# Another order of ScalarE, VectorE, GpSimd and transfer requests in one unit of work and in units 1 to 6 of a fused attention and feed-forward kernel

## The chip, the cores and the metric

The kernel runs on one core of one Trainium2 chip. A core has five engines that each work through a queue of their own in order: TensorE (PE in the profile; PEld are its weight loads), VectorE (DVE), ScalarE (ACT), GpSimd (POOL) and SyncE (SP), which here issues nearly all transfers. They meet through semaphores. The metric is the time of one execution on the device in microseconds; lower is better. The kernel before takes 911.8 us (median of three runs, 911.2 to 911.83).

## The reference

Attention with pooled keys and values, and behind it a feed-forward layer, all in float32. There are 8 batches, 8 heads, 576 tokens and 64 elements per head; the layer has 512 inputs and 2048 hidden elements.

```python
k_p = k.reshape(B, H, 72, 8, D).mean(axis=3)
v_p = v.reshape(B, H, 72, 8, D).mean(axis=3)
scores = scale * np.matmul(q, k_p.transpose(0, 1, 3, 2))
scores = scores - np.max(scores, axis=-1, keepdims=True)
attn = np.exp(scores)
attn = attn / (np.sum(attn, axis=-1, keepdims=True) + 1e-09)
x = np.matmul(attn, v_p).transpose(0, 2, 1, 3).reshape(B * S, H * D)
h = x @ w_in
s = np.sin(alpha * h)
g = h + s * s / (alpha + 1e-09)
out = g @ w_out
```

## The kernel before

The program has two stages. In the first, unit u (0 to 7) computes the hidden layer of batch u, and in the gaps between its products it carries the attention of batch u + 1. In the second stage `outputs` multiplies g, which was parked in device memory (`g_bridge`), with w_out. Both matrix products use seven block products in place of eight (Strassen and Winograd): sums of weight blocks (`as1`, `as2`, `as4`, and `a21` overwritten with a difference) and sums of x blocks (the `home` tiles) are made by GpSimd and VectorE, and TensorE multiplies them.

`hidden` (L1030) works in four parts J, each a quarter of the hidden elements. A part owns four banks of PSUM, b1, b5, b6 and b7. After the first product ScalarE copies b1 into b6 (`copy(G.b6, G.b1)`), TensorE goes on adding to b6, ScalarE copies b6 into b7, and so on: in the profile these are the `ACT COPY PS<-PS 128x512` rows, and TensorE can't start the products `PS<-home,as` on b6 before the copy is there. Then ScalarE takes sin and square (`s`), VectorE adds h, p5 and s into `h`, and SP stores `h` to `g_bridge`. In units 1 to 6 the products 1 and 5 of the later parts are themselves split once more (`inner_product`, L1146); its step d is an add on VectorE, `PS<-PS,m` in the profile, for which the next product waits.

`first_batch` (L1192) does the attention of batch 0 and the first weights, ahead of unit 0. `carry(u)` (L1286) gives the list of what unit u carries, by slot: for u = 0 among other things `sum_v_rows`, the rest of batch 0's attention, `pairs_q` for batch 1, `load_w_in_part` 2 and 3, the weight sums `combine_w_in` of parts 1 to 3, the transposes of queries and keys (`q_t`, `k_t`), `two_scores` (products), `two_shifts` (row maxima and subtraction, `mx` and `ex` in the profile), `exp`, `norm` (sums `sm` on VectorE, the scaling `ex<-ex,sm` on GpSimd), `turn` (VectorE's transposes `tr<-ex`), `move` (the transfers `aM<-tr`) and `turn_q` (the queries of the last tokens, transfers `q<-tr`). `pool_k` and `pool_v` are GpSimd's sums over eight rows (`kvin<-kvin`, `kp`, `vm`). `pairs_q` (L315) copies the queries of one batch on ScalarE, five copies of 128x512 (`q<-q`), from a tile that one request of 1024 KB brings. `refine` improves a reciprocal of alpha on VectorE (`t`, `c`), which ScalarE's square reads.

The order of the work is written in a table. Between `begin` and `flush` every operation is only recorded (class `Order`, L30; this is why all rows of the profile have the line L156). `flush` (L139) computes which operation needs which, and then sorts the queue of each engine but TensorE by a number; TensorE keeps the order of the program text. The number is `unit * 5406` plus the entry of the table `PLAN` for the operation's key: the part (`0` for unit 0, `u` for units 1 to 6, `7`, `8` for units on their own, `a` for the first batch) and the label of the function that `carry` named, followed by the running number of the operation under this key. The entries read like times in hundredths of a microsecond. SP is a queue like the others; a request waits until the one eight places before it has landed.

Of the kernel before, what the change touches and what calls it, by code (L numbers as in the profile page):

```python
# [189 lines left out]
0.: 0 0 0 0 2004 0 0 0 0 0 0 0 0 2591 0 0 0 0 2633 2696 2690 2746 2694 4180 0 0 0 0 2990 2765 2695 0 0 0 0 4153 2764 4401 0 0 0 0 2763 2775 5075 4488 2772 4489 4208 4777 5545 5542 0 0 0 0 4486 0 0 0 0 0 0 0 0 5073 0 0 0 0 5074 5077 5078 5136 5128 4798 0 0 0 0 4778 5409 5572 0 0 0 0 4796 5357 5425 0 0 0 0 5441 5440 5444 5442 5445 5789 4850 4851 5556 5752 0 0 0 0 5377 0 0 0 0 0 0 0 0 5443 0 0 0 0 5529 5702 5615 5794 5792 4861 0 0 0 0 4848 5852 5795 0 0 0 0 4856 5798 6403 0 0 0 0 5800 5797 8483 7999 5855 5799 4866 8188 5773 5766 0 0 0 0 5850 0 0 0 0 0 0 0 0 6301 0 0 0 0 6335 8687 8002 8723 8716 8405 0 0 0 0 8176 8733 8863 0 0 0 0 8200 8734 9669 0 0 0 0 8732 9668 8997 9675 9343 9670 9566 9825 10996 11157  # L190
0.sum_v_rows : 0 0 0 0 0 0 0 0 1974
0.rest_q : 0 0 0 0 1975
0.a_head : 0 0 0 0 1976 0 0 0 0 2136 0 0 0 0 2002
0.values : 0 0 0 0 0 0 2137 2144 2006 2007
0.score : 0 0 0 0 0 0 0 0 2189 2204 2182 2208
0.sums_of_x : 2164 2206 8538 8549
0.load_w_in_part : 1725 2031 2255 1019 5540 683 1828 1956
0.pairs_q : 2299 2612 2003 2005 2755
0.call : 5175 3333
0.combine_w_in : 3139 3158 3332 3331 3336 3338 3501 3383 3834 5996 5169 8465  # L200
0.q_t : 0 0 0 0 2213 0 0 0 0 2222 0 0 0 0 4487 0 0 0 0 5071 0 0 0 0 5070
0.k_t : 0 0 0 2219 0 0 0 8471
0.two_scores : 0 0 0 0 0 0 0 0 0 0 0 0 0 0 0 0 0 0 0 0 0 0 0 0 0 0 0 0 0 0 0 0 4127 4194 3335 4124 4125 4128 0 0 0 0 0 0 0 0 0 0 0 0 0 0 0 0 0 0 0 0 0 0 0 0 0 0 0 0 0 0 0 0 0 0 0 0 0 0 0 0 4211 4774 4214 4776
0.load_v : 5536 5537 1606 4600 660 507 3399 3602 3718
0.<lambda> : 3161 3335 3337 3367 8457 8458 8459 7637 8463 8464 0 0 0 0 0 0 0 0 0 0 0 0 7576 8000 6318 6990
0.exp : 2675 5072 5076 5120 5336
0.load_q : 5538 5546 5543
0.norm : 4511 4787 3660 4784 4797 3752 4811 4812 4427 4801 4803 3793
# [20 lines left out]
u.load_k : 376 5758  # L229
u.pool_k : 3087 3088 3091 8469 8471 8477  # L230
u.move : 5779 5774 5773 5769 5764 5766 5771 5767 5777 5775 5776 5762 5778 5763 5768 5770
u.turn_q : 7643 7606 7969 6332 6330 6292 6328 6255 6334 6333 6335 6339 6336 6340 5895 6338 6331 6426 6472
u.all_values : 0 0 0 0 0 0 0 0 0 0 8016 0 0 0 0 0 0 0 0 0 0 0 0 0 0 0 0 0 0 8512 8520 8579 8519 8521 8564 8577 8557 8551
u.k_t : 0 0 0 8267
# [1486 lines left out]
```

## Time and profile before

| | |
|---|---|
| median of three runs | 911.8 us |
| profiled execution | 915.4 us |
| its span, first to last instruction | 913.4 us |
| mean granted TensorE clock | 0.996 |
| TensorE busy | 898.0 us, 98% |
| VectorE busy | 667.4 us, 73% |
| ScalarE busy | 457.9 us, 50% |
| GpSimd busy | 196.6 us, 22% |

The span is the time between the first and the last instruction of the profiled execution; the rest of its 915.4 us lies around it. In a row of the timeline stand start and duration in microseconds, the engine, the operation, the tile written and the tiles read (numbers left out), the shape, how many instructions of the kind came in a row, and in brackets how long the engine had been idle before and what released it. The releaser is inferred. A row that covers several instructions (x8) has the time from the start of the first to the end of the last. The view by windows gives the busy time of TensorE, its weight loads, VectorE, ScalarE and GpSimd in each stretch, with the number of instructions, and then the granted clock of TensorE (1.00 is full), the share of the transfer engines, and GB/s.

### The profile page before, as it was taken

The page shows a single profiled execution, that of the slowest core. Times are in us where ns is not written, and L with a number is a line of the kernel's source. Part 1 is how long each engine was busy: PE and PEld are TensorE (multiplying, and loading weights), DVE is VectorE, ACT ScalarE, POOL GpSimd, SP SyncE. Part 2 cuts the span into 40 slices and gives each one's busy share as a digit, 9 for nine tenths or more (in the row PEclk, how much of TensorE's full clock was granted, in tenths as well). Part 3 has the DMA queues.
Part 4 walks back from the last instruction along what each step waited for, and adds up shares of the span by engine and source line. Part 5 has one row for each costly group of instructions (what it writes and reads, how often), then busy time and mean ns, then how long its engine had stood idle before and what let it go on. Part 6 is the DMA issues. An engine that isn't in the chain of part 4 may idle for free.

```text
span 913.4 us, 18293 instructions
## 1 busy us (share of the span) xinstructions
PE 898.0 (98%) x7122; PEld 818.5 (90%) x7122; DVE 667.4 (73%) x1029; ACT 457.9 (50%) x1112; POOL 196.6 (22%) x232
## 2 busy tenths in 40 slices
PE   8899999999999999999999999999999999999998
PEld 5687888888888788888888899999999999999998
DVE  7465866858587585764279589979787878878884
ACT  5486876877768687787796631111111112112111
POOL 4579754424445144220000000000000000000000
PEclk9899999999999999999999999999999999999999
DMA  9947676586666766343727237352527262626211
GB/s 259 228 131 195 193 209 202 158 229 187 194 184 172 206 191 184 122 133 127 266 93 248 93 103 227 115 145 70 181 39 191 57 183 77 183 66 195 66 39 40
DMA packets 128748, 141.14 MB, mean 155 GB/s; under 512 B 46920, under 2 KB 95704, under 8 KB 128664
## 3 DMA queue, kind: packets, MB, share of 16 engines
q1 hardware_dynamic: 125880, 137.88, 52.3%
q10 hardware_dynamic: 2784, 2.11, 0.9%
q8 instruction: 56, 0.92, 0.4%
q14 instruction: 28, 0.23, 0.1%
HBM read 75.37 MB, written 47.19 MB: 134 GB/s over the span
## 4 chain that ended last, share of the span: by engine, by line
PE 91%; DMA 3%; DVE 2%; SPq 2%; issue 0%; ACT 0%; DVEq 0%
PE PS L156 91%; SPq L156 2%; DMA a<-in_moe_w_in_dram 2%; DMA home<-in_k_dram 1%; DMA kvin<-in_v_dram 1%; DVE h L156 1%; DVE tr L156 0%; DMA q<-tr 0%; DVE ex L156 0%; DVE PS L156 0%; DVE mx L156 0%; DVE sm L156 0%; ACT L156 0%; ACT q L156 0%; DVE c L156 0%
## 5 line engine op out<-in xcount | busy, mean ns | idle before, releaser
L156 ACT COPY PS<-PS 128x144 f32<-128x144 f32 (+4 forms) x312 | 114.4, 369 | 296.6 <-PE PS L156 282.2
L156 PE MATMUL PS<-home,a 128*128 128x256 f32 (+1 forms) x1080 | 253.2, 376 | 1.4 <-DVE h L156 0.5
L156 PEld LDWEIGHTS PS<-home,a 128*128 128x128 f32 x1080 | 196.8, 191 | 30.1 <-issue 4.6
L156 PE MATMUL PS<-home,as 128*128 128x256 f32 (+1 forms) x792 | 188.6, 374 | 4.0 <-ACT PS L156 4.0
L156 PEld LDWEIGHTS PS<-home,as 128*128 128x128 f32 x792 | 144.4, 192 | 21.9 <-ACT PS L156 4.4
L156 PE MATMUL PS<-s,wb 128*128 128x144 f32 x896 | 119.1, 286 | 0.0
L156 ACT ACTIVATE s<-s,c 128x256 f32<-128x256 f32 (+1 forms) x216 | 116.7, 577 | 4.5 <-DVE c L156 2.1
L156 PEld LDWEIGHTS PS<-s,wb 128*128 128x128 f32 x896 | 113.7, 190 | 0.1
L156 POOL TENSOR_TENSOR cc<-cc,cb 128x576 f32<-128x576 f32 x1 | 2.0, 1983 | 504.9 <-DVE cb L156 504.9
L156 ACT ACTIVATE s<-PS,al 128x256 f32<-128x256 f32 x144 | 64.5, 471 | 33.5 <-PE PS L156 33.3
L156 DVE TENSOR_TENSOR h<-PS,s 128x512 f32<-128x512 f32 x72 | 49.0, 681 | 36.3 <-ACT s L156 35.9
L156 ACT ACTIVATE s<-h,al 128x256 f32<-128x256 f32 x144 | 68.6, 507 | 12.8 <-DVE h L156 12.7
L156 PE MATMUL PS<-s,a 128*128 128x144 f32 x512 | 73.2, 286 | 0.0
L156 PE MATMUL PS<-r,wb 128*128 128x144 f32 x512 | 73.2, 286 | 0.0
L156 DVE TENSOR_TENSOR h<-PS,p 128x512 f32<-128x512 f32 x72 | 49.0, 680 | 25.0 <-ACT p L156 12.7
L156 POOL TENSOR_TENSOR kvin<-kvin 96x768 f32<-96x768 f32 (+3 forms) x42 | 66.0, 1573 | 5.5 <-DMA kvin<-in_v_dram 4.8
L156 PEld LDWEIGHTS PS<-r,wb 128*128 128x128 f32 x512 | 67.1, 190 | 0.1
L156 PEld LDWEIGHTS PS<-s,a 128*128 128x128 f32 x512 | 67.0, 190 | 0.0
L156 DVE TENSOR_TENSOR h<-h,s 128x1024 f32<-128x1024 f32 x36 | 50.2, 1394 | 18.9 <-ACT s L156 18.9
L156 PE MATMUL PS<-x,wb 128*128 128x144 f32 x384 | 54.9, 286 | 0.0
L156 PE MATMUL PS<-s,we 128*128 128x144 f32 x384 | 54.9, 286 | 0.0
L156 POOL TENSOR_TENSOR ex<-ex,sm 128x576 f32<-128x576 f32 (+1 forms) x28 | 35.3, 1272 | 86.3 <-DVE sm L156 75.0
(170 smaller groups left out, 1309.2 us busy)
## 6 DMA issues: line engine op xcount, KB each, us to landing
g_bridge<-h SPq DMA_DIRECT2D x72, 512.0 KB
r<-g_bridge SPq DMA_DIRECT2D x31, 1152.0 KB
out_dram<-o SPq DMA_DIRECT2D x122, 72.0 KB
kvin<-in_k_dram SPq DMA_DIRECT2D x14, 576.0 KB
q<-in_q_dram SPq DMA_DIRECT2D x7, 1024.0 KB
kvin<-in_v_dram SPq DMA_DIRECT2D x14, 512.0 KB
aM<-tr SPq DMA_DIRECT2D x54, 92.0 KB
aM<-tr SPq DMA_DIRECT2D x54, 88.0 KB
```

Of the source, the lines that this page charges most:

```text
L156: t.f(*t.a, **t.k)
```

## The change

Only entries of `PLAN` change: those of part `0` (unit 0) and of part `u` (units 1 to 6). The entries of the first batch's own part `a`, of units 7 and 8 and of the second stage stay. So the same instructions run on the same data; TensorE's program is the same, instruction by instruction, and the queues of ScalarE, VectorE, GpSimd and SP have another order from the point where unit 0 is mixed into the first batch, through unit 6. A selection of the changed lines follows; all other labels under `0` and `u` have new entries too, in the same manner.

```diff
--- before
+++ after
@@ -187,51 +187,51 @@
-0.: 0 0 0 0 2004 0 0 0 0 0 0 0 0 2591 0 0 0 0 2633 2696 2690 2746 2694 4180 0 0 0 0 2990 2765 2695 0 0 0 0 4153 2764 4401 0 0 0 0 2763 2775 5075 4488 2772 4489 4208 4777 5545 5542 0 0 0 0 4486 0 0
...
-0.load_w_in_part : 1725 2031 2255 1019 5540 683 1828 1956
-0.pairs_q : 2299 2612 2003 2005 2755
-0.combine_w_in : 3139 3158 3332 3331 3336 3338 3501 3383 3834 5996 5169 8465
-0.q_t : 0 0 0 0 2213 0 0 0 0 2222 0 0 0 0 4487 0 0 0 0 5071 0 0 0 0 5070
-0.load_v : 5536 5537 1606 4600 660 507 3399 3602 3718
-0.exp : 2675 5072 5076 5120 5336
-0.norm : 4511 4787 3660 4784 4797 3752 4811 4812 4427 4801 4803 3793
-0.turn : 4814 4799 4810 4813 4838 4828 4821 4815 4849 4816 4807 4809
-0.inner_w_in : 8468 8490 8496 8500 5172 8471 5173 8481 8462 8472 8488 13874 3551 6818 8498 8483 8461 8492 8489 13884 8460 8474 8466 13864
-u.: 0 0 0 0 3590 0 0 0 0 4268 0 0 0 0 4270 4271 4543 4542 4452 0 0 0 0 0 0 4541 4401 0 0 0 0 4544 4474 5061 5025 0 0 4545 0 0 0 4475 0 0 4478 5098 5307 0 0 0 0 0 0 5305 5253 5308 5311 5309 5306
...
-u.inner_x : 3074 3089 3085 3093 3073 3076 3079 3078
-u.load_v : 354 348 347 133 138 135 3070 3080 3081
-u.norm : 4477 4499 3095 4479 4481 3096 4480 5279 8457 5241 5242 3097
-u.turn : 4563 5283 5281 5251 5287 5328 5286 5680 5285 5379 5280 6064
-u.pool_v : 3061 3064 3067 3069
-u.pool_k : 3087 3088 3091 8469 8471 8477
...
+0.: 0 0 0 0 2019 0 0 0 0 0 0 0 0 2024 0 0 0 0 2913 3322 3421 3323 3866 3963 0 0 0 0 2221 3347 3870 0 0 0 0 2757 3975 3873 0 0 0 0 3372 3724 5445 5443 3958 3871 4146 4307 4958 4692 0 0 0 0 3872 0 0
...
+0.load_w_in_part : 1702 412 2367 1749 4594 4503 2068 2255
+0.pairs_q : 2023 2022 2025 2342 3324
+0.combine_w_in : 3105 3107 3117 3116 3109 3111 3145 3143 3157 3344 3341 3345
+0.q_t : 0 0 0 0 2173 0 0 0 0 2210 0 0 0 0 3582 0 0 0 0 3941 0 0 0 0 4009
+0.load_v : 4495 4560 4825 4643 4631 4511 3242 3335 3339
+0.exp : 2668 5441 5444 5453 5451
+0.norm : 4154 4265 3222 4266 4293 3231 4725 4726 3332 4436 4469 3331
+0.turn : 4801 4800 4502 4803 4802 4804 4788 4794 4795 4798 4799 4756
+0.inner_w_in : 3110 3367 3334 8466 3115 3185 8470 8464 3237 3333 8500 8469 3148 3338 8487 8492 3352 8499 8472 8501 8465 8474 3376 8486
+u.: 0 0 0 0 4277 0 0 0 0 4283 0 0 0 0 4289 4290 4294 4424 4476 0 0 0 0 0 0 4293 4295 0 0 0 0 4296 4444 5355 4965 0 0 4297 0 0 0 4445 0 0 4478 5353 5358 0 0 0 0 0 0 5013 5351 5362 5361 5359 5360
...
+u.inner_x : 3056 3067 3062 3082 3057 3074 3061 3079
+u.load_v : 5544 5556 152 163 161 149 3088 3090 3091
+u.norm : 4477 4479 3085 4480 4667 3092 4481 4482 3087 4484 4487 3089
+u.turn : 4483 4486 4674 4673 4488 4489 4671 4669 4670 4672 5161 5326
+u.pool_v : 3055 3065 3069 3076
+u.pool_k : 3083 3084 8458 8457 8459 8460
...
```

In words, what moves in the stretch of the first batch and unit 0:

- On ScalarE the copies b6 from b1 (2004, now 2019) and b7 from b6 (2591, now 2024) of the first part: the former stood behind the first `pairs_q` copy, and now stands ahead of all of them.
- On SP the request for the queries of batch 1 goes from place 22 to 19; four requests for value rows (`vr`, 64 KB each) go from places 11, 14, 23 and 34 to 32, 36, 37 and 41; the weight requests between them close up and change places.
- On VectorE several `ex<-PS,mx` and `h<-PS,p` move ahead of `h<-h,s` and of row maxima, and the refinement of the reciprocal moves back.
- On GpSimd small sums of weight blocks for the inner products of unit 1 (`q<-a`, `q<-as`, `last<-a`) are spread over unit 0 among the weight sums, and value sums (`vr`, `vz`) move back.

In units 1 to 6 the reciprocals of the softmax sums and some of the transposes `tr<-ex` change places with the h adds on VectorE, single sin and square operations change places on ScalarE, and on GpSimd the pooling of the next values (`kvin<-kvin`) moves from early in a unit to between the softmax scalings.

More of the change, by code (lines that the diff above doesn't have):

```diff
@@ L191 @@
[L191 to L196, printed above, removed]
-0.load_w_in_part : 1725 2031 2255 1019 5540 683 1828 1956
-0.pairs_q : 2299 2612 2003 2005 2755
-0.call : 5175 3333
-0.combine_w_in : 3139 3158 3332 3331 3336 3338 3501 3383 3834 5996 5169 8465
-0.q_t : 0 0 0 0 2213 0 0 0 0 2222 0 0 0 0 4487 0 0 0 0 5071 0 0 0 0 5070
@@ L202 @@
-0.k_t : 0 0 0 2219 0 0 0 8471
-0.two_scores : 0 0 0 0 0 0 0 0 0 0 0 0 0 0 0 0 0 0 0 0 0 0 0 0 0 0 0 0 0 0 0 0 4127 4194 3335 4124 4125 4128 0 0 0 0 0 0 0 0 0 0 0 0 0 0 0 0 0 0 0 0 0 0 0 0 0 0 0 0 0 0 0 0 0 0 0 0 0 0 0 0 4211 4774 4214 4776
-0.load_v : 5536 5537 1606 4600 660 507 3399 3602 3718
-0.<lambda> : 3161 3335 3337 3367 8457 8458 8459 7637 8463 8464 0 0 0 0 0 0 0 0 0 0 0 0 7576 8000 6318 6990
-0.exp : 2675 5072 5076 5120 5336
-0.load_q : 5538 5546 5543
-0.norm : 4511 4787 3660 4784 4797 3752 4811 4812 4427 4801 4803 3793
@@ L209 @@
-0.load_k : 5547 5548
-0.two_shifts : 4775 4785
-0.turn : 4814 4799 4810 4813 4838 4828 4821 4815 4849 4816 4807 4809
-0.norm_rest : 2608 4126 4951 3334 3160
-0.move : 5697 5558 5554 5751 5553 5552 5617 5550 5557 5551 5549 5555 5796 5793 5791 5790
-0.a_rest : 0 0 0 0 0 5856
-0.inner_w_in : 8468 8490 8496 8500 5172 8471 5173 8481 8462 8472 8488 13874 3551 6818 8498 8483 8461 8492 8489 13884 8460 8474 8466 13864
-0.turn_q : 4873 4870 7364 5756 5758 5755 5759 5761 5762 5765 5763 5769 5757 5771 5770 5764 5767 5772 5768
@@ L228 @@
-u.pool_v : 3061 3064 3067 3069
-u.load_k : 376 5758
-u.pool_k : 3087 3088 3091 8469 8471 8477
[L231 to L234, printed above, removed]
+0.: 0 0 0 0 2019 0 0 0 0 0 0 0 0 2024 0 0 0 0 2913 3322 3421 3323 3866 3963 0 0 0 0 2221 3347 3870 0 0 0 0 2757 3975 3873 0 0 0 0 3372 3724 5445 5443 3958 3871 4146 4307 4958 4692 0 0 0 0 3872 0 0 0 0 0 0 0 0 5442 0 0 0 0 5446 5449 5447 5450 5448 4414 0 0 0 0 4268 5463 5455 0 0 0 0 4309 5454 5456 0 0 0 0 5461 5458 5466 5460 5465 5459 4806 4808 5553 5554 0 0 0 0 5452 0 0 0 0 0 0 0 0 5457 0 0 0 0 5462 5468 5467 5470 5472 4809 0 0 0 0 4805 5475 5473 0 0 0 0 4807 5486 5481 0 0 0 0 5474 5471 5493 5494 5478 5477 4810 4814 5566 5577 0 0 0 0 5476 0 0 0 0 0 0 0 0 5483 0 0 0 0 5488 5485 7852 5490 7859 6412 0 0 0 0 4815 9692 9684 0 0 0 0 5606 9690 9686 0 0 0 0 9673 9685 9691 9693 9694 9687 9482 9619 10966 10965
@@ new lines @@
+0.sum_v_rows : 0 0 0 0 0 0 0 0 2015
+0.rest_q : 0 0 0 0 2018
+0.a_head : 0 0 0 0 2016 0 0 0 0 2136 0 0 0 0 2017
+0.values : 0 0 0 0 0 0 2143 2153 2020 2021
+0.score : 0 0 0 0 0 0 0 0 2154 2164 2156 2158
+0.sums_of_x : 2170 2155 8255 8520
+0.load_w_in_part : 1702 412 2367 1749 4594 4503 2068 2255
+0.pairs_q : 2023 2022 2025 2342 3324
+0.call : 3337 3108
+0.combine_w_in : 3105 3107 3117 3116 3109 3111 3145 3143 3157 3344 3341 3345
+0.q_t : 0 0 0 0 2173 0 0 0 0 2210 0 0 0 0 3582 0 0 0 0 3941 0 0 0 0 4009
@@ new lines @@
+0.k_t : 0 0 0 2214 0 0 0 7334
+0.two_scores : 0 0 0 0 0 0 0 0 0 0 0 0 0 0 0 0 0 0 0 0 0 0 0 0 0 0 0 0 0 0 0 0 2224 2668 2220 3781 2222 2580 0 0 0 0 0 0 0 0 0 0 0 0 0 0 0 0 0 0 0 0 0 0 0 0 0 0 0 0 0 0 0 0 0 0 0 0 0 0 0 0 4151 4300 4308 4361
+0.load_v : 4495 4560 4825 4643 4631 4511 3242 3335 3339
+0.<lambda> : 3336 3340 3343 3348 3346 3347 7189 3368 3378 3386 0 0 0 0 0 0 0 0 0 0 0 0 5489 5487 5491 5484
+0.exp : 2668 5441 5444 5453 5451
+0.load_q : 5101 4628 4662
+0.norm : 4154 4265 3222 4266 4293 3231 4725 4726 3332 4436 4469 3331
@@ new lines @@
+0.load_k : 4654 5544
+0.two_shifts : 4156 4267
+0.turn : 4801 4800 4502 4803 4802 4804 4788 4794 4795 4798 4799 4756
+0.norm_rest : 2219 2223 3287 3342 3113
+0.move : 5547 5550 5546 5234 5342 5375 5549 5310 5545 5551 5552 5548 5479 5482 5469 5464
+0.a_rest : 0 0 0 0 0 5480
+0.inner_w_in : 3110 3367 3334 8466 3115 3185 8470 8464 3237 3333 8500 8469 3148 3338 8487 8492 3352 8499 8472 8501 8465 8474 3376 8486
+0.turn_q : 4812 4813 4811 5556 5562 5560 5561 5565 5559 5564 5563 5575 5571 5570 5568 5572 5573 5574 5576
@@ new lines @@
+0.all_values : 0 0 0 0 0 0 0 0 0 0 5492 0 0 0 0 0 0 0 0 0 0 0 0 0 0 0 0 0 0 7848 7905 7875 7714 7779 5917 9668 9672 7867
+u.sums_of_x : 3292 3125 7984 8493
+u.: 0 0 0 0 4277 0 0 0 0 4283 0 0 0 0 4289 4290 4294 4424 4476 0 0 0 0 0 0 4293 4295 0 0 0 0 4296 4444 5355 4965 0 0 4297 0 0 0 4445 0 0 4478 5353 5358 0 0 0 0 0 0 5013 5351 5362 5361 5359 5360 4490 4536 5643 5639 4952 0 0 0 0 5352 5354 0 0 5357 0 0 5356 0 0 0 4485 0 0 0 0 5366 5367 5363 5370 5369 4668 0 0 0 0 5364 5365 0 0 4643 6143 6441 0 0 5368 0 0 0 4666 0 0 4996 6542 6437 0 0 0 0 0 0 6468 6439 6621 6628 6541 6504 5519 5845 5784 5782 6164 0 0 0 0 6424 6467 0 0 6469 0 0 6458 0 0 0 5501 0 0 0 0 6623 6619 6620 6627 6624 5820 0 0 0 0 6622 6626 0 0 5588 6631 6632 0 0 6625 0 0 0 5794 0 0 5896 6639 6640 0 0 0 0 0 0 6630 6636 7357 6951 6635 6638 7569 7979 5802 10951 6629 0 0 0 0 6633 6634 0 0 6785 0 0 6637 0 0 0 7458 0 0 0 0 6642 6641 7412 9679 7535 8323 0 0 0 0 7982 9682 9680 0 0 0 0 8170 9685 9684 0 0 0 0 9687 9688 9692 9686 9690 9691 9848 9849 10963 10965
@@ new lines @@
+u.two_scores : 0 0 0 0 0 0 0 0 0 0 0 0 0 0 0 0 0 0 0 0 0 0 0 0 0 0 0 0 0 0 0 0 3201 3234 3212 3244 3223 3256 0 0 0 0 0 0 0 0 0 0 0 0 0 0 0 0 0 0 0 0 0 0 0 0 0 0 0 0 0 0 0 0 0 0 0 0 0 0 0 0 3748 3805 3773 4351
+u.inner_x : 3056 3067 3062 3082 3057 3074 3061 3079
+u.two_shifts : 3798 3799
+u.load_v : 5544 5556 152 163 161 149 3088 3090 3091
+u.load_q : 5650 5638 5783
+u.exp : 4292 4291 4504 4464
+u.norm : 4477 4479 3085 4480 4667 3092 4481 4482 3087 4484 4487 3089
+u.turn : 4483 4486 4674 4673 4488 4489 4671 4669 4670 4672 5161 5326
@@ L235 @@
+u.pool_v : 3055 3065 3069 3076
+u.load_k : 383 5640
+u.pool_k : 3083 3084 8458 8457 8459 8460
+u.move : 5657 5652 5647 5649 5656 5651 5645 5641 5710 5654 5653 5642 5655 5644 5646 5648
+u.turn_q : 7974 7971 7976 5791 5792 5790 5787 5788 5794 5793 5795 5800 5796 5797 5798 5799 5801 5785 5786
+u.all_values : 0 0 0 0 0 0 0 0 0 0 6643 0 0 0 0 0 0 0 0 0 0 0 0 0 0 0 0 0 0 9676 7517 9673 9678 9672 9675 9674 9677 9681
+u.k_t : 0 0 0 8476
 7.: 42508 42507 42505 42506 0 0 0 0 42507 0 0 0 0 0 0 0 0 42508 0 0 0 0 42509 42510 42511 42514 42515 42390 0 0 0 0 42388 42512 42520 0 0 0 0 42389 42513 42523 0 0 0 0 42517 42519 42521 42525 42522 42528 42391 42393 42510 42509 0 0 0 0 42516 0 0 0 0 0 0 0 0 42524 0 0 0 0 42526 42530 42531 42536 42535 42395 0 0 0 0 42392 42534 42539 0 0 0 0 42394 42537 42543 0 0 0 0 42550 42538 42547 42546 42552 42541 42399 42396 43585 43586 0 0 0 0 42542 0 0 0 0 0 0 0 0 42549 0 0 0 0 42545 42553 42555 42554 42563 42404 0 0 0 0 42398 42560 42562 0 0 0 0 42403 46237 42566 0 0 0 0 46281 42565 46238 42567 46325 46236 46819 46817 43587 43588 0 0 0 0 42564 0 0 0 0 0 0 0 0 46239 0 0 0 0 46419 46421 46706 46807 46809 46823 0 0 0 0 46818 46808 46756 0 0 0 0 46820 46811 46810 0 0 0 0 46814 46813 46817 46812 46816 46815 46826 46827 43589 43590
```

8 lines of the change are left out of this document (removed).

## The prediction

> **What bounds the kernel now.** I read the page first: which engine is busy, and the clock row.
>
> ```profile
> PE 898.0 (98%) x7122; PEld 818.5 (90%) x7122; DVE 667.4 (73%) x1029; ACT 457.9 (50%) x1112; POOL 196.6 (22%) x232
> ...
> PEclk9899999999999999999999999999999999999999
> ```
>
> TensorE is busy for 898.0 of 913.4 us, so all other engines together can give back 15.4 us, and nothing that leaves the TensorE program alone can give more, except through the clock. The clock row has one digit of 8, early. The view by windows says where the idle time and the low clock are (window, its length, PE busy; PEclk is the third figure from the end of a row).
>
> ```profile
> 0.00:20.00 20.00, 17.75 (x224) 10.79 (x224) 13.95 (x35) 11.05 (x22) 6.95 (x16) 1.00 0.97 264
> 20.00:40.00 20.00, 15.29 (x90) 11.08 (x91) 7.44 (x17) 8.01 (x18) 13.37 (x13) 0.84 1.06 250
> 40.00:120.00 80.00, 78.69 (x712) 66.12 (x711) 55.33 (x94) 61.56 (x129) 63.06 (x76) 1.00 0.65 176
> 120.00:400.00 280.00, 277.25 (x2325) 237.58 (x2324) 196.07 (x337) 213.28 (x514) 110.85 (x126) 1.00 0.64 182
> 400.00:880.00 480.00, 479.88 (x3538) 464.02 (x3539) 377.11 (x521) 159.15 (x416) 0.36 (x1) 1.00 0.45 135
> ```
>
> Idle are 2.25 us in the first 20, 4.71 in the next 20, 1.31 from 40 to 120 (unit 0), 2.75 from 120 to 400 (units 1 to 5), 0.12 after that. The 20 to 40 slice also ran at a mean clock of 0.84. TensorE's waits, from the view of waits (total, times, longest):
>
> ```profile
> PE PS L156 <- ACT PS L156: 4.0, 1, 4.0
> PE PS L156 <- DVE PS L156: 2.5, 6, 0.4
> ```
>
> One wait of 4.0 us on ScalarE stands out; then come six of about 0.42 us on VectorE, and a few single ones. These two rows lie in the part of the program that the change reorders. ScalarE's timeline shows the large one (start, duration, idle time before it and its releaser), and TensorE's what it did to the products:
>
> ```profile
> 25.80 0.58 ACT L156 COPY aM<-PS 64x512 f32<-64x512 f32 x1 [0.29 <-PE PS L156]
> 32.91 0.62 ACT L156 COPY q<-q 128x512 f32<-128x512 f32 x1 [6.54 <-DMA a<-in_moe_w_in_dram]
> 33.54 0.57 ACT L156 COPY PS<-PS 128x512 f32<-128x512 f32 x1
> ```
>
> ```profile
> 25.60 1.89 PE L156 MATMUL PS<-home,as 128*128 128x256 f32 x8
> 27.42 1.09 PE L156 MATMUL PS<-aM,vm 64*64 64x512 f32 x8
> 28.44 1.13 PE L156 MATMUL PS<-aM,vz 32*128 32x512 f32 x4
> 29.50 0.72 PE L156 MATMUL PS<-h,q 64*64 64x72 f32 x16
> 34.17 3.78 PE L156 MATMUL PS<-home,as 128*128 128x256 f32 x8 [3.95 <-ACT PS L156]
> 37.74 3.19 PE L156 MATMUL PS<-home,a 128*128 128x256 f32 x8
> 40.77 0.49 PE L156 MATMUL PS<-ident,q 128*128 128x128 f32 x3
> ```
>
> From the timeline of VectorE and of SP's requests, two rows more:
>
> ```profile
> 29.65 0.76 DVE L156 SCALAR_TENSOR_TENSOR home<-PS,home 128x256 f32<-128x256 f32 x2 [3.60 <-PE PS L156]
> ...
> 32.86 0.37 SPq L156 DMA_DIRECT2D a<-in_moe_w_in_dram  x1
> ```
>
> TensorE is done with everything it can do at 30.21 and waits for a bank copy, b6 from b1 (`PS<-PS`, 0.57 us). That copy's source was written by the eight products that started at 25.60; it could run then. But it is queued on ScalarE behind a copy of the second batch's queries (`pairs_q`, 0.62 us), and ScalarE stands 6.54 us until the 1 MB query transfer has landed. The row names a transfer of weights; by the code, the copy reads the queries, and the request on SP that waits for the query transfer (eight requests behind it) is the one issued at 32.86, so landing was about 32.85.
>
> The second thing to see: the products after the wait take 3.78 and 3.19 us, against 1.89 for the same eight at 25.60. The clock by windows:
>
> ```profile
> 30.00:33.50 3.50, 0.21 (x8) 0.06 (x2) 0.49 (x3) 0.59 (x1) 3.34 (x4) 1.00 1.13 233
> 33.50:34.00 0.50, 0.00 (x0) 0.00 (x0) 0.00 (x0) 0.49 (x2) 0.38 (x1) 0.54 1.15 304
> 34.00:40.00 6.00, 5.83 (x14) 4.68 (x15) 2.95 (x8) 4.10 (x9) 0.00 (x0) 0.50 0.99 295
> 40.00:40.50 0.50, 0.50 (x3) 0.41 (x2) 0.00 (x0) 0.48 (x2) 0.00 (x0) 0.63 1.09 174
> ```
>
> It fell to half 3.3 us into the wait and came back 6 us after TensorE resumed. Lost: 5.83 x 0.50 + 0.50 x 0.37 = 3.1 us (by the product rows, 3.78 + 3.19 - 2 x 1.89 = 3.2). So this one wait costs 3.95 + 3.1 = 7.05 us.
>
> [...]
>
> **The change, part by part.** The TensorE program is the same, so the sum is over waits.
>
> *ScalarE at 26 to 36 us.* In the changed plan the bank copy (due 2019, was 2004) and the next one (2024, was 2591) are sorted against `pairs_q` at 2022, 2023, 2025, 2342 and 3324 (was 2003, 2005, 2299, 2612, 2755), and ScalarE's order becomes: last aM copy, bank copy b6 from b1, two copies of x sums (`home`), then the query copies. The bank copy can start when the aM copy ends, 25.80 + 0.58, and its source at 25.60 + 1.89 / 2: about 26.5 to 27.5, ahead of 30.21. The products behind it also read home sums that VectorE makes at 29.65 + 0.42; that holds. Stall and half clock go: -3.95 and -3.1. Bounds: nothing gained if a new wait over 3.3 us arises at once; all of it if none does.
>
> *What is late next.* The next operands of TensorE are the transposes of the same queries, at 40.77 now, so at 33.7. With landing at 32.85 the first two query copies (0.62 each) end at 34.1: 0.4 late. But the query request also moves, from place 22 to 19 on SP, with 384 KB less ahead of it; at the 250 GB/s of the slice that is 1.5 us earlier, and then it is in time. Behind these copies VectorE's two q copies and the kblk copy follow; by the same walk they end within 0.4 us of their need. Between 0 and 0.4 late; I put this into the margin term below.
>
> *Other requests on SP.* The four small vr requests go behind the weights (places 32 to 41 instead of 11 to 34), the first weights of part 0 come 128 KB earlier or 192 KB later (0.5 to 0.8 us at 250 GB/s), and the last heads of the first queries 256 KB later (1 us). TensorE reads the late ones where the first 20 us already wait on transfers (2.25 us idle there), so I allow -0.5 to +0.8 and take 0.
>
> *VectorE in unit 0.* `ex<-PS,mx` and `h<-PS,p` move ahead of work that held them up:
>
> ```profile
> 49.46 0.91 PE L156 MATMUL PS<-home,a 128*128 128x256 f32 x3 [0.40 <-DVE ex L156]
> ...
> 63.28 0.91 PE L156 MATMUL PS<-home,a 128*128 128x256 f32 x3 [0.52 <-DVE h L156]
> ...
> 97.85 0.72 PE L156 MATMUL PS<-kblk,q 64*64 64x72 f32 x30 [0.40 <-DMA q<-tr]
> ```
>
> The add `h<-h,s`, the longest on VectorE, now stands behind the `h<-PS,p` that the products at 63.28 need, so 0.52 goes. Of the 0.40 before 49.46 I take half: TensorE arrives 7 us earlier, and VectorE's refinement of 1/alpha (c, t) is now ahead of that ex. The 0.40 at 97.85 ends a chain of rearranging transfers that now start earlier and stand together on SP: gone. Together -1.1.
>
> *Margins in unit 0.* With TensorE 7 us ahead, work that had slack loses it. ScalarE's square now waits for c (refined later), so an h add ahead of the scores, three bank copies and POOL's weight sums run closer to their need; walking the queues with the durations that each instruction had in this trace leaves 0 to 0.2 us at five places. I charge +0.6 (0 to 2).
>
> *POOL in unit 0.* Several small sums of W2 go ahead of the last part's weight sums. By the same walk the one that is needed first ends about 1 us ahead of its need. Free, if the softmax sums that POOL waits for come as early as VectorE's order allows; else up to 1 us.
>
> *Units 1 to 6.* The six waits on VectorE are alike, one in each unit; the fourth:
>
> ```profile
> 287.66 0.18 DVE L156 RECIPROCAL sm<-sm 128x8 f32<-128x8 f32 x1
> 287.77 0.74 DVE L156 STREAM_TRANSPOSE tr<-ex 128x32 f32<-128x32 f32 x2
> 288.44 0.39 DVE L156 TENSOR_TENSOR PS<-PS,m 128x256 f32<-128x256 f32 x1
> ...
> 288.89 0.38 PE L156 MATMUL PS<-home,q 128*128 128x128 f32 x1 [0.43 <-DVE PS L156]
> ```
>
> The add `PS<-PS,m` of the inner product is held up by a reciprocal (0.18) and two transposes (0.74). In the changed order these three stand behind it; in exchange three other transposes move ahead, but in front of two h adds that wait for TensorE anyway. By the walk the add ends about 0.5 us sooner: the wait goes or shrinks. Other copies in the units have little slack, and single ScalarE operations move in front of some. So six times between -0.43 and +0.3; I take half of the gain, -1.25.
>
> **Sum**: -3.95 - 3.1 - 1.1 + 0.6 - 1.25 = -8.8 us. The profiled execution took 915.4 us (span 913.4, 2.0 around it), 3.6 above the median of 911.8; so 906.6 for a profiled run, and 903.0 for the median, if the timed runs hold the same wait and the same half clock.
>
> **Rivals.**
>
> 1. *The clock term is not in the timed runs.* The profiled run is 3.6 us longer than they are, close to the 3.1 us of the clock: a wait shorter by half a microsecond might not trip it. Then the gain is 5.7: 906.1. For it: that difference, and a wait only 0.6 us longer than the 3.3 after which the clock fell. Against: taking a profile may itself lengthen a run. [...]
> 2. *The wait moves to the query transposes.* If landing is no earlier and the copies and VectorE's q and kblk copies queue up, 1 to 4 us come back at 34 us: 904 to 907, say 907 with further margins lost.
> 3. *The units give it back (slower).* VectorE now has two transposes of the third softmax group in front of its h adds and `PS<-PS,m`, and they wait for POOL's norm:
>
> ```profile
> 238.17 2.35 POOL L156 TENSOR_TENSOR kvin<-kvin 128x1024 f32<-128x1024 f32 x1
> ...
> 280.36 2.26 POOL L156 TENSOR_TENSOR ex<-ex,sm 128x576 f32<-128x576 f32 x2 [11.35 <-DVE sm L156]
> ```
>
> POOL's pooling of the values (2.35), early in the unit before, now stands between the norms. By the walk the third group's norm ends at 281.3, 2.2 us before VectorE reaches the transposes. A delay of POOL beyond 2.2 us goes into TensorE, six times; it takes 2.2 + 0.2 + 7.55 / 6 = 3.7 us to cancel the gain of 7.55 elsewhere, and one late transfer of values under that pooling would do it. At 4.2 us: 911.8 - 7.55 + 6 x 1.8 = 915. Against it: POOL is idle 11 us just before.
> 4. *No change*: 2 and 3 in part, 911.
>
> **Numbers.** Forecast 0.54 (903.0, own range 900.8 to 905: the upper end of all waits gone, -10.9, and 2 us more of margins lost); rival 1, 0.14; rival 2, 0.12; no change, 0.07; slower, 0.13. 0.2% is 1.8 us, about what a measurement here can tell from no change. Faster: 0.54 + 0.14 + 0.12 = 0.80; same 0.07; slower 0.13. The range runs from 900.5 to 910.5, which leaves out the slower rival and part of the fourth.
>
> **What would show it.** In the profile after: no TensorE wait on ScalarE near 30 us, PEclk 9 in the second slice, query copies starting at 31 to 33 with TensorE at work beside them; `h` and `ex` waits gone from the list; waits on `DVE PS` fewer or shorter. Wrong: a new wait on `ACT q`, `DVE kblk` or `DMA` between 30 and 45 us, or a row of six equal waits in the units on `DVE h`, `DVE PS` or `ACT PS` that is longer than 0.43.

## The result and the profile after

The changed kernel takes 907.05 us (median of seven runs, 904.59 to 910.48); the kernel before, beside it on the same chip, 912.71 (seven runs, 911.2 to 916.2). The ratio is 0.993 with a 95% interval of 0.9903 to 0.9957: faster by 5.7 us. A later comparison on another chip gave 905.44 against 913.76, ratio 0.9909 (0.9888 to 0.993): faster by 8.3 us. The forecast was 903.0 and -8.8 us. The profiled execution after took 904.6 us, span 902.8.

Two rows of the page, busy time and clock:

```profile
PE 893.7 (99%) x7122; PEld 816.0 (90%) x7122; DVE 663.8 (74%) x1029; ACT 459.4 (51%) x1112; POOL 202.4 (22%) x232
...
PEclk9999999999999999999999999999999999999999
```

The span fell by 10.6 us. TensorE's idle time (span less busy) went from 15.4 to 9.1, so 6.3 of it; its busy time fell by 4.3, though the same products ran: the half clock is gone (1.00 from 20 to 40 us, was 0.84). The same windows as before:

```profile
0.00:20.00 20.00, 17.83 (x224) 10.88 (x224) 13.98 (x35) 11.08 (x22) 8.22 (x17) 1.00 0.98 274
20.00:40.00 20.00, 18.79 (x182) 14.36 (x183) 12.47 (x26) 9.95 (x20) 15.33 (x15) 1.00 1.08 266
40.00:120.00 80.00, 78.71 (x658) 66.38 (x657) 58.10 (x101) 63.16 (x136) 63.48 (x76) 1.00 0.60 169
120.00:400.00 280.00, 279.87 (x2350) 240.90 (x2349) 190.13 (x333) 219.10 (x527) 113.36 (x123) 1.00 0.66 188
400.00:880.00 480.00, 480.00 (x3566) 465.20 (x3565) 377.89 (x518) 153.27 (x402) 0.00 (x0) 1.00 0.43 132
```

Idle per row, before and after: 2.25 and 2.17, 4.71 and 1.21, 1.31 and 1.29, 2.75 and 0.13, 0.12 and 0. So two stretches gave nearly all of it: the stall (-3.5) and the units (-2.6). Unit 0 from 40 us on gave nothing. TensorE's waits (total, times, longest) show why:

```profile
PE PS L156 <- DVE home L156: 1.3, 2, 1.0
...
PE PS L156 <- DMA q<-tr: 0.8, 1, 0.8
...
PE PS L156 <- DVE sm L156: 0.5, 1, 0.5
```

The wait on ScalarE of 4.0 and the six on `DVE PS` are gone. So are `ex` and `h`; in their place stand `home` 0.97, `sm` 0.46, and a `q<-tr` that is longer (0.83, was 0.40). The timelines of ScalarE and TensorE where the stall was:

```profile
26.00 0.59 ACT L156 COPY PS<-PS 128x512 f32<-128x512 f32 x1
...
31.67 1.13 ACT L156 COPY q<-q 128x512 f32<-128x512 f32 x2
```

```profile
31.20 1.56 PE L156 MATMUL PS<-home,as 128*128 128x256 f32 x6 [0.97 <-DVE home L156]
32.60 1.89 PE L156 MATMUL PS<-home,a 128*128 128x256 f32 x8
34.32 1.04 PE L156 MATMUL PS<-ident,q 128*128 128x128 f32 x8
```

The bank copy runs at 26.00 (was 33.54), the products follow at full speed (1.89 for eight, was 3.19), and the query copies run beside them. The transposes of the queries, feared to be late next, don't wait. The fourth unit, where the add `PS<-PS,m` came late before, in the timeline of VectorE and TensorE:

```profile
278.84 0.43 DVE L156 TENSOR_TENSOR PS<-PS,m 128x256 f32<-128x256 f32 x1 [0.64 <-PE PS L156]
279.18 0.19 DVE L156 RECIPROCAL sm<-sm 128x8 f32<-128x8 f32 x1
...
279.50 0.38 PE L156 MATMUL PS<-home,q 128*128 128x128 f32 x2
```

The add now starts when TensorE has written its input, the reciprocal stands behind it, and the next product finds it done.

### The profile page after: what moved, and what is told of

Same layout as the page of the kernel before. It is cut to its first block, busy times and chain, and to the rows that moved or that the text cites. A ratio compares the mean times of both kernels' runs of the same rounds, so it can differ in the third digit from the quotient of the medians.

```text
span 902.8 us, 18295 instructions
## 1 busy us (share of the span) xinstructions
PE 893.7 (99%) x7122; PEld 816.0 (90%) x7122; DVE 663.8 (74%) x1029; ACT 459.4 (51%) x1112; POOL 202.4 (22%) x232
## 4 chain that ended last, share of the span: by engine, by line
PE 96%; ACT 1%; DVE 1%; SPq 1%; issue 0%; DMA 0%; DVEq 0%
PE PS L156 96%; ACT s L156 1%; SPq L156 1%; DVE h L156 0%; ACT PS L156 0%; DMA q<-tr 0%; DVE t L156 0%; ACT q L156 0%; ACT L156 0%; DVE PS L156 0%; DVE home L156 0%; DVE o L156 0%; DVE cc L156 0%; ACT h L156 0%; ACT home L156 0%
## 5 line engine op out<-in xcount | busy, mean ns | idle before, releaser
L156 ACT ACTIVATE s<-h,al 128x256 f32<-128x256 f32 x144 | 70.5, 510 | 12.5 <-DVE h L156 12.4
L156 POOL TENSOR_TENSOR kvin<-kvin 96x768 f32<-96x768 f32 (+3 forms) x42 | 69.7, 1659 | 17.4 <-DMA kvin<-in_k_dram 16.7
L156 DVE TENSOR_TENSOR h<-h,s 128x1024 f32<-128x1024 f32 x36 | 48.1, 1336 | 14.1 <-ACT s L156 13.2
L156 DVE TENSOR_TENSOR PS<-PS,m 128x256 f32<-128x256 f32 x36 | 15.5, 432 | 56.0 <-PE PS L156 41.0
```

The costliest lines, as they stand in the source:

```text
L156: t.f(*t.a, **t.k)
```

## The experiments

The first theory was the prediction's: ScalarE's one place in the queue, with the half clock that follows, is most of the gain, and the rest are small margins. The rival: the four queues' new orders are worth something only together. Runs e1 to e4, e5 to e9 (there is no e8) and e10 to e12 were each made together, on one chip; each ratio is to the kernel before on the same chip.

**e1: the bank copy alone.** Before, with the query copies behind it.

```diff
-0.pairs_q : 2299 2612 2003 2005 2755
+0.pairs_q : 2008 2612 2009 2010 2755
```

> The kernel before, with three copies of the second batch's queries placed on ScalarE behind the bank copy b6 from b1 and the two home copies; nothing else moves. Theory (the stall and the half clock are this one queue position): TensorE's wait on ScalarE at 30 us goes, the clock stays at 1.00 from 30 to 41 us, and the query transposes wait up to 1.5 us because the request on SP has not moved; 3 to 6 us faster than before. Rival (the query transfer bounds this stretch whatever ScalarE does): the wait appears at the transposes instead, less than 1.5 us gained.

Measured: 916.52 against 913.76, ratio 1.0019 (1.0002 to 1.0036). No gain. TensorE's timeline:

```profile
30.34 1.97 PE L156 MATMUL PS<-home,as 128*128 128x256 f32 x8
...
35.71 0.66 PE L156 MATMUL PS<-ident,q 128*128 128x128 f32 x4 [1.24 <-ACT q L156]
...
61.39 5.41 PE L156 MATMUL PS<-home,a 128*128 128x256 f32 x16 [4.66 <-DVE h L156]
```

The stall at 30 and its half clock are gone, as forecast (the clock is 1.00 from 30 to 41 us), for a wait of 1.24 on the query copies. But at 61 a new wait of 4.66 arises, with half clock behind it: the 16 products took 5.41 us, the next 16 took 3.62. VectorE's and GpSimd's timelines there:

```profile
53.70 7.03 DVE L156 TENSOR_TENSOR h<-h,s 128x1024 f32<-128x1024 f32 x1
60.66 0.68 DVE L156 TENSOR_TENSOR h<-PS,p 128x512 f32<-128x512 f32 x1
```

```profile
53.22 1.26 POOL L156 TENSOR_TENSOR as<-a,as 128x512 f32<-128x512 f32 x1
...
58.38 1.27 POOL L156 TENSOR_TENSOR kvin<-kvin 128x512 f32<-128x512 f32 x1
```

Between these two rows of GpSimd lie three more sums, with no gap (`kvin` 2.35, `a` 1.27, `q` 0.46). The add `h<-h,s` took 7.03 us, against 2.89 in the profile before:

```profile
59.74 2.89 DVE L156 TENSOR_TENSOR h<-h,s 128x1024 f32<-128x1024 f32 x1
```

The median of its 36 instances there is 1.22. In both profiles it ended 1.1 us after GpSimd's last sum of a series without a gap (60.73 after 59.65; 62.63 after 61.53). With the stall gone VectorE reaches the add 6 us earlier, but the series ends only 1.9 us earlier, so 6 us of it are still to come, where 1.8 were before. So the first theory fell as to the time, and a second was formed: VectorE's add is held until GpSimd pauses. e5 tests it.

**e2: unit 0's part alone.** All entries with the key `0` as in the change, those with `u` as before:

```diff
-0.move : 5697 5558 5554 5751 5553 5552 5617 5550 5557 5551 5549 5555 5796 5793 5791 5790
+0.move : 5547 5550 5546 5234 5342 5375 5549 5310 5545 5551 5552 5548 5479 5482 5469 5464
...
 u.load_v : 354 348 347 133 138 135 3070 3080 3081
```

> The kernel before with the changed entries of unit 0 alone; units 1 to 6 keep their old order. Theory: everything but the six waits of 0.42 us is gained, so it lies 2.5 us above the changed kernel, and its trace still shows six waits on VectorE's PS<-PS,m. Rival (the old order of the units suffers where unit 0 runs into unit 1): more than 4 us above the changed kernel.

Measured: 930.59, ratio 1.0175 (1.015 to 1.02): 17 us slower. TensorE's timeline and SP's requests:

```profile
90.97 1.12 PE L156 MATMUL PS<-aM,vm 64*64 64x512 f32 x6 [9.02 <-DMA aM<-tr]
...
117.51 0.80 PE L156 MATMUL PS<-x,q 128*128 128x128 f32 x2 [6.39 <-POOL x L156]
```

```profile
81.21 0.64 SPq L156 DMA_DIRECT2D vr<-in_v_dram  x1
81.89 7.34 SPq L156 DMA_DIRECT2D aM<-tr  x8
```

Unit 0's transfers `aM<-tr` now stand behind requests of unit 1 whose entries are old and which come too early for them: before the `vr` requests at 79.29 SP had stood 9.0 us, until GpSimd's sum `vz` that reads their tile had ended (79.26). TensorE stands 9.02 us, and 6.39 more at 117 on a sum that GpSimd makes late. The numbers of two units that meet in one queue belong together. The reverse, only the entries of `u`, has no run: the queues would then wait on each other in a circle.

**e3: the change, once more**, on the chip of e1, e2 and e4, unaltered.

> The changed kernel unaltered, for a second profile. Its seven runs spread from 904.6 to 910.5. Theory (the spread comes from transfers in the first 100 us that land at different times): the stretch from 120 us on takes the same time in both profiles within 0.5 us, and the difference lies in waits before that. Rival (the clock): runs above 908 show a lower mean clock and a stretch at half clock.

Measured: 905.44, ratio 0.9909 (0.9888 to 0.993), the second result given above. The expectation's question stays half open. From 120 us on the two profiles agree (0.15 and 0.13 us idle up to 400), but both are of the fastest run of their set. For the rival, the clock, speaks that of the 19 runs of the changed kernel and of e4 the four above 908 us show a mean clock of 0.997 or 0.998, and of the other 15 only one does (907.01).

**e4: the new wait at 31.20.** In the profile after, VectorE's and GpSimd's timelines ahead of it:

```profile
28.98 0.42 DVE L156 SCALAR_TENSOR_TENSOR home<-PS,home 128x256 f32<-128x256 f32 x1 [3.60 <-PE PS L156]
29.33 1.48 DVE L156 TENSOR_TENSOR t<-c 128x16 f32<-128x16 f32 x1
30.73 0.41 DVE L156 SCALAR_TENSOR_TENSOR home<-PS,home 128x256 f32<-128x256 f32 x1
```

```profile
28.97 2.88 POOL L156 TENSOR_TENSOR kvin<-kvin 96x768 f32<-96x768 f32 x2
```

A step of the refinement (`t<-c`, 128x16) has come between the two `home` adds, and beside GpSimd's sums it takes 1.48 us. Before, it stood behind both and took 0.17:

```profile
30.32 0.17 DVE L156 TENSOR_TENSOR t<-c 128x16 f32<-128x16 f32 x1
```

GpSimd ran there too, and in e10, the same kernel as before, it took 1.36. So its length varies; what the new place adds is that an add which TensorE needs stands behind it. The edit to the changed kernel puts it behind both again:

```diff
-0.values : 0 0 0 0 0 0 2143 2153 2020 2021
+0.values : 0 0 0 0 0 0 2143 2151 2020 2021
```

> The changed kernel with one entry altered: the first step of the reciprocal's refinement (t<-c) goes behind the two adds of x sums on VectorE instead of between them. In the profile after it took 1.48 us there, beside GpSimd, and TensorE waited 0.97 us at 31.2. Theory: that wait goes, and with it 0.9 to 1.1 us of the time. Rival: the query transposes wait instead, under 0.3 us gained.

Measured: 904.42, ratio 0.9901 (0.9876 to 0.9926), 1.0 below e3 with overlapping intervals. In its profile the wait near 31 is gone:

```profile
30.19 0.76 DVE L156 SCALAR_TENSOR_TENSOR home<-PS,home 128x256 f32<-128x256 f32 x2 [3.60 <-PE PS L156]
30.86 1.17 DVE L156 TENSOR_TENSOR t<-c 128x16 f32<-128x16 f32 x1
```

The place of the wait is confirmed; its worth of about 1 us isn't separable in the times. In this profile another wait is longer, 1.58 us for `q<-tr` at 94.7 (0.46 in e3's).

**e5: e1 with a pause of GpSimd.** GpSimd's three last value sums go behind four softmax scalings.

```diff
-0.load_v : 5536 5537 1606 4600 660 507 3399 3602 3718
+0.load_v : 5536 5537 1606 4600 660 507 4428 4429 4430
```

> The kernel with only the query copies moved (the run before it in this document), and on GpSimd the three sums of the next values (kvin 128x1024, kvin 128x512, vm) moved from the middle of unit 0 to behind four softmax scalings. In the profile of the former, VectorE's add h<-h,s took 7.03 us at 53.7, while GpSimd ran without a gap until 59.65, and TensorE waited 4.7 us for the add behind it. Theory (VectorE's add with both inputs in SBUF gets through only when GpSimd pauses): the add takes under 4 us, TensorE's wait there falls to 0.5 to 2 us and no stretch at half clock follows; 3 to 6 us faster than the former. Rival (the add waits for a transfer of h, not for GpSimd): it still ends near 60.7, no gain.

Measured: 917.49, ratio 1.0039 (1.0025 to 1.0052). VectorE's timeline:

```profile
53.45 1.44 DVE L156 TENSOR_TENSOR h<-h,s 128x1024 f32<-128x1024 f32 x1
```

7.03 became 1.44, with GpSimd idle from 53.80, and the wait near 61 is gone. Only GpSimd's order differs from e1, so it is GpSimd that held the add there; whether it must pause is taken up in e6. The time did not follow, since the gain went to the next place, again a wait with half clock behind it (3.75 us for eight products, 1.97 in e1). TensorE's and ScalarE's timelines:

```profile
79.20 3.75 PE L156 MATMUL PS<-home,as 128*128 128x256 f32 x8 [5.01 <-ACT PS L156]
```

```profile
76.16 0.51 ACTq L156 DMA_DIRECT2D aM<-tr  x1
76.72 0.47 ACT L156 ACTIVATE s<-PS,al 128x256 f32<-128x256 f32 x1 [6.09 <-DMA aM<-tr]
```

ScalarE, too, issues a transfer here, and had done no other work for 6.09 us when it was out. That the delayed value sums hold up the transfers ahead of it is a reading of the queues; no run isolated it.

**e6: unit 0's new order on ScalarE and VectorE only** (GpSimd and SP as before).

```diff
-                t.at = n if e == "PE" else t.unit * UNIT.get(t.key[0][0], 0) + self.plan.get(t.key, 0)
+                plan = self.plan_after if e in ("ACT", "DVE") else self.plan
+                t.at = n if e == "PE" else t.unit * UNIT.get(t.key[0][0], 0) + plan.get(t.key, 0)
```

(`plan_after` is `PLAN` with the changed lines of key `0`; shortened here.)

> The kernel before with the changed order of unit 0 on ScalarE and VectorE alone; GpSimd and SP keep the old order, and so do units 1 to 6. Theory (VectorE's h<-PS,p ahead of the long add is what keeps the gain): no wait of 4 us near 60, the six waits of 0.42 us remain; 5 to 7 us faster than before, 907 to 909. Rival (GpSimd's old order starves VectorE anyway): under 2 us faster.

Measured: 923.72, ratio 1.0103 (1.0082 to 1.0123). Its timeline (the added table moves the line to L160, here and in e7):

```profile
55.92 7.09 DVE L160 TENSOR_TENSOR h<-h,s 128x1024 f32<-128x1024 f32 x1
...
64.12 5.38 PE L160 MATMUL PS<-home,as 128*128 128x256 f32 x16 [4.17 <-DVE h L160]
```

With GpSimd's old series the add is held again, 7.09 us. In the changed kernel, with GpSimd's new order, the same add takes 2.13:

```profile
55.25 2.13 DVE L156 TENSOR_TENSOR h<-h,s 128x1024 f32<-128x1024 f32 x1
```

GpSimd's rows beside it:

```profile
55.15 1.15 POOL L156 TENSOR_TENSOR ex<-ex,sm 128x576 f32<-128x576 f32 x1 [1.34 <-DVE sm L156]
56.26 1.44 POOL L156 TENSOR_TENSOR q<-as 128x128 f32<-128x128 f32 x1
```

The add did not wait for a pause here. It got in behind one GpSimd sum (it ended at 57.38, that sum at 56.30), and the next one, of a kind that takes 0.46 elsewhere, took 1.44. So "held until GpSimd pauses" is too strong as a rule; what decides between the two cases no run shows. What lets the earlier VectorE run is GpSimd's new order, which the prediction called free. Which of its moves does it was not separated.

The add isn't all of e6's loss. A second wait of the same size follows where unit 0's new order on ScalarE meets unit 1's old one:

```profile
113.47 0.77 PE L160 MATMUL PS<-x,q 128*128 128x128 f32 x2 [4.45 <-ACT PS L160]
```

**e7: the change without ScalarE's part** (the same switch: VectorE, GpSimd and SP by the changed table, ScalarE by the old one, in all units).

> The changed kernel with ScalarE's queue in the old order, in unit 0 and in units 1 to 6; VectorE, GpSimd and SP as changed. Theory (the large stall is ScalarE's queue): TensorE waits for ScalarE's bank copy near 30 us, 2.5 to 4 us, since the query request is earlier on SP by 1.5 us, and the six waits in the units are gone; 1 to 4 us faster than before. Rival (the stall comes from the query request's place on SP): no wait over 1 us there, and as fast as the changed kernel.

Measured: 912.42, ratio 0.9979 (0.9963 to 0.9995). TensorE's and ScalarE's timelines:

```profile
34.14 3.78 PE L160 MATMUL PS<-home,as 128*128 128x256 f32 x8 [2.15 <-ACT PS L160]
...
71.39 3.42 PE L160 MATMUL PS<-home,as 128*128 128x256 f32 x8 [3.79 <-ACT PS L160]
```

```profile
32.89 0.62 ACT L160 COPY q<-q 128x512 f32<-128x512 f32 x1 [4.74 <-DMA a<-in_moe_w_in_dram]
```

The stall and the half clock are back (0.50 from 33.5 to 40 us), and a second one comes at 71 (eight products in 3.42). The units keep their gain: TensorE is busy 279.46 of the 280 us from 120 on. So ScalarE's order is worth about 6 us where the other three are new (-8.3 in e3 against -2.0 here, each to the kernel before on its chip), while its main step was worth nothing where they are old (e1). The query transfer landed at about 32.75 here, by the prediction's own sign (the request eight places behind it on SP), hardly earlier than before: its request stands three places earlier, but went out at 18.06, and before at 18.26. In the profile after it went out at 15.62 and landed by 29.07. With the old order on ScalarE and that landing, a query copy (0.62) and the bank copy (0.57) would end at 30.26, 0.7 us after TensorE gets there (29.55): an estimate. So a rival stays untested: in runs where the transfer comes that early, the request's new place on SP alone may take most of the stall away.

**e9: two requests off the path.** e4, with two `vr` requests moved back, in unit 1 from between the `q<-tr` requests to behind them, and GpSimd's sums of them with them. The entries are those of `u`, so units 1 to 6 all have them.

```diff
-u.load_v : 5544 5556 152 163 161 149 3088 3090 3091
+u.load_v : 5544 5556 152 173 172 149 3088 3090 3091
...
-u.pool_v : 3055 3065 3069 3076
+u.pool_v : 3080 3081 3082 3082
```

> The kernel with t<-c moved, and two small requests for value rows put behind the last q<-tr requests on SP (from units 1 on), with GpSimd's sums of these rows behind its x sums. In the profile of the former TensorE waited 1.58 us at 94.7 for q<-tr. Theory (two requests of 0.7 us in front of them make the last q<-tr late): that wait falls below 0.4, 1 to 1.5 us faster. Rival (landing takes as long wherever they stand): the wait stays over 1 us.

Measured: 903.38, ratio 0.9878 (0.9859 to 0.9896), the fastest of all, 1.2% below the kernel before. In its profile no wait on `q<-tr` is left (1.58 in e4's), but the same products wait 0.99 for a VectorE add:

```profile
94.42 1.62 PE L156 MATMUL PS<-kblk,q 64*64 64x72 f32 x80 [0.99 <-DVE home L156]
```

So the two requests weren't the only thing late there, and the 1.0 us below e4 lies within the intervals.

**e10 to e12: the kernel before, unaltered, three more profiles.** What was open: whether the half clock is in every run, and for how long. In e1, e2, e5, e6 and e7 each stretch at half clock lasted 3.4, 6.8 or 10.2 us (e7's first, from 33.36 to 40.19, 6.83; the mean clock from 40 to 120 us was 0.98 in e1 and e7, 0.96 in e5 and e6, 0.91 in e2).

> The kernel before, unaltered, profiled once more: TensorE again idles from about 30.2 to 34.2 us. Theory A (fixed windows): in the profiles so far each stretch at half clock lasted 3.41, 6.83 or 10.24 us, whole multiples of 3.41, and ended with the first window of 3.41 us that TensorE was busy all through; the windows run free of the program. Then the clock falls at another time than 33.54, anywhere from about 31.6 to 35.0, comes back exactly 6.8 us later if it fell before TensorE resumed and 3.4 us later if it fell after, and costs between 1.7 and 3.4 us by that phase. Theory B (the prediction's reading): the clock falls 3.3 us after TensorE went idle, at 33.5, and comes back about 6 us after it resumed, and costs 3.1 us every time.

> The same kernel a second time, for another phase of the windows. Theory A: a fall at a time that differs from the other profiles by up to 3.4 us, a length of 3.41 or 6.83. Theory B: 33.5 and 40.4 again, within 0.3.

> The same kernel a third time. Theory A: as for the other two, and among four profiles (with the first one) the times of the fall differ by more than 1 us and the loss by more than 0.5 us. Theory B: four times alike.

Measured: 914.37, 914.39 and 915.65 us for the profiled runs. Windows of 0.5 us where the clock falls and returns (the clock is the third figure from the end), of e10:

```profile
32.00:32.50 0.50, 0.00 (x0) 0.00 (x0) 0.00 (x0) 0.21 (x1) 0.50 (x1) 0.86 1.10 203
39.00:39.50 0.50, 0.50 (x4) 0.41 (x3) 0.00 (x0) 0.50 (x2) 0.00 (x0) 0.82 1.14 156
```

and of e12:

```profile
34.50:35.00 0.50, 0.21 (x1) 0.21 (x2) 0.00 (x0) 0.50 (x2) 0.00 (x0) 0.55 0.74 219
37.50:38.00 0.50, 0.50 (x3) 0.40 (x2) 0.50 (x3) 0.00 (x0) 0.00 (x0) 0.53 0.87 295
```

Windows that lie wholly on one side show 0.50 (e10, 33.5 to 38 us) or 1.00 (e12, 30 to 34 and 38 to 41). So a window with clock 0.86 was at full speed for (0.86 - 0.5) / 0.5 = 72% of it, and in e10 the clock fell at 32.36 and came back at 39.18: 6.82 us. In e12 it fell at 34.55 and came back at 37.97: 3.42. In e11 it was 33.62 to 40.45 (6.83), in the first profile 33.54 to 40.37 (6.83). TensorE resumed at 33.55, 34.79, 35.14 and 34.17. Half the time from there to the return is lost (at 0.50 eight products take 3.78, at 1.00 1.89): 2.8, 1.6, 2.7 and 3.1 us. So theory A holds, but for one point: in e12 the clock fell before TensorE resumed and still came back after 3.4, not 6.8. In these 3.4 us TensorE was idle for 0.24; in the first profile it was idle for 0.63 of the first 3.4 behind the fall, and the clock came back after the second.

The lengths are alike (6.82 and 6.83) or half of that (3.42). In e7 the second return can be put at about 74.3: eight products took 3.42 from 71.39, against 1.99 behind a wait at full clock, so the half clock lasted 2 x 1.43 into them. That is an estimate; it lies ten times 3.41 behind the first return (40.19). How far into its wait the clock falls differs: 3.3 us in the first profile, 2.3 in e10 (32.36, idle from 30.08), 4.0 in e12, and in e7 at 33.36, only 1.4 us into a wait of 2.15. What decides whether it falls, no run shows.

## Why the prediction was right and where it wasn't

The sign, the place and most of the mechanism were right; the sum was near since the units gave more than forecast and unit 0 less, and that these cancel is luck. The time came out 2.4 to 4.1 us above the forecast, inside the range.

- **ScalarE at 26 to 36 us, the stall (-3.95):** right. The copy ran at 26.00, near the forecast 26.5; the slice gave 3.5, since the wait of 0.97 stands in it and one of 0.47 at 23.74 went. In e1 ScalarE's order alone ended this stall; whether SP's new order would have done so too is open (e7). "That holds", said of the `home` sums, is the step that failed here: it took the second add at its old distance from the first, and `t<-c` came between them, at 1.48 us.
- **The half clock (-3.1):** right in kind, mis-sized. Four profiles of the kernel before lost 1.6 to 3.1, 2.5 in the mean, so rival 1 was right that the profiled run was at the upper end. The clock is not absent from the timed runs: the mean granted clock is 0.9966 over 17 runs before and 0.9987 over six after (e3), 3.1 and 1.2 us of the span (in the profile after 1.04 us are lost, all of it from 900.72 on, behind TensorE's last product, which ends at 898.45). The rival's reasoning by a wait only just long enough was wrong: in e10 the wait was 3.47, half a microsecond shorter, and 2.8 us were lost all the same.
- **What is late next:** no wait at the query transposes in the changed kernel, as forecast; in e1, without the rest of the change, 1.24. Rival 2 did not come about. That the earlier request brings the data 1.5 us earlier was mis-sized, and no fixed figure: by the request eight places behind, the transfer landed at 29.07 after, 30.83 in e3 and 32.75 in e7, so 3.8, 2.0 and 0.1 earlier than the 32.86 of before.
- **Other requests on SP (0):** right in the first profile, 2.25 and 2.17 idle in the first 20 us, but likely about 1 us too low. The seven profiles with SP's old order (the first, e1, e5, e6, e10 to e12) have 1.88 to 2.77 idle there, 2.3 in the mean; the six with the new one (the first after, e2, e3, e4, e7, e9) 2.17 to 4.34, 3.3 in the mean. The wait on the first queries (`q<-in_q_dram`), which the prediction saw come 1 us later, is 0.45, 1.22, 1.28 and 2.12 in e3, e4, e9 and e7, and 0 to 0.7 with the old order.
- **VectorE in unit 0 (-1.1) and margins (+0.6):** the waits on `ex` and `h` are gone, but `q<-tr` grew by 0.43 and `sm` came with 0.46, so 40 to 120 us gave 0.02. With the 0.97 ahead of it, margins cost about 2.3 (0.97 + 0.46 + 0.83), not 0.6; the bound of 2 was nearly right.
- **POOL in unit 0 ("free"):** right by the list of waits, which has none on GpSimd, but it missed what matters. The walk gave each instruction the duration it had before; `h<-h,s` took 2.89, 2.13, 7.03 or 1.44 us by what GpSimd did beside it. That e1 alone gives nothing can't be seen in such a walk.
- **Units 1 to 6 (-1.25):** mis-sized, -2.6. All six waits went wholly; "half of the gain" was caution without a row. Rival 3, the price of GpSimd's norms, did not come about: 0.13 us idle in 280.
- **The sum against the median:** -8.8 was made against a profiled run 3.6 us above the median, and the whole clock term was carried over. The two profiles differ by 10.8, the medians by 5.7 and 8.3; the profile after (904.6) is the fastest of its seven runs. Of the 10.6 us of span, 3.5 are the stall, 2.6 the units, 3.1 the clock, 0.2 the two ends; 1.2 of TensorE's busy time I can't place.

What stays open: why the seven runs after spread by 5.9 us (904.59 to 910.48). Those at 908.8 and 910.5 show a clock of 0.997, at least 2.3 us of the span lost, against 1.04 in the profile after; so a half clock likely still comes in some runs of the changed kernel; but one of 907.9 shows 1.0. The lower end of the forecast's own range, 911.8 - 10.9, is 900.9, not 900.8.

## What to carry to other kernels

A stall that goes sends every other engine's work to meet at new times: one queue's fix alone was worth nothing (e1), two queues cost 9 us (e6), one unit's entries without its neighbour's 17 (e2), all together saved 6 to 8. When you walk queues by old durations, mark each instruction whose duration changed with its company, and treat it as a wait; and cost a half clock as a range (1.6 to 3.1 us over four profiles of one kernel here), not as the figure of one profile.

## What the runs showed of the hardware

- A VectorE add of 128x1024 with both inputs in SBUF can be held by GpSimd's sums: it took 7.03 us (e1) and 7.09 (e6) in a series without a gap, 1.44 with GpSimd idle (e5), and 2.13 in the changed kernel, where it got in between two sums. In e1 it was under way while five GpSimd instructions ran in a row (the one that ran when it started and four more) and ended 1.1 us after the last of them; in the changed kernel it ended 1.1 us after the first. The 128x512 adds with one input in PSUM (`h<-PS,p`, `h<-PS,s`) took 0.63 to 0.69 us in all 144 instances of the profile before, 36 of which ran beside GpSimd instructions. A 128x16 operation took 0.17 to 1.62 us (1.62 in e3) beside the same GpSimd sums.
- Half clock came in lengths of 3.42, 6.82 and 6.83 us, up to 10.2 in e2, where TensorE idled 9.02 us (mean clock 0.91 from 40 to 120 us). In the last 3.4 us before it ended, TensorE was busy throughout in the first profile and in e10, and all but 0.24 us in e12. It came behind a wait of 2.15 us (e7); one of 1.24 passed without (e1).
